# First MoE of a fused attention and two-MoE kernel: joining and casting the float64 weights at other turns

## The chip, the cores and the metric

One core of one Trainium2 chip runs the whole program in one launch. The metric is the device time of an execution in microseconds; lower is better.

## The reference

Three layers follow each other on 4 sequences of 576 tokens: causal attention with a local or a strided mask, a first MoE layer that is a plain two-matrix feed-forward net behind a layer norm, and a second MoE layer that sends each token to one of eight experts. The change touches the first MoE alone. Its two weight matrices are float64 (a float32 array times a float64 scalar), everything else is float32:

```python
def _moe_ref(x, g_ln, w_ch1, w_ch2) -> np.ndarray:
    mu = np.mean(x, axis=-1, keepdims=True)
    var = np.mean((x - mu) ** 2, axis=-1, keepdims=True)
    xn = (x - mu) / np.sqrt(var + 1e-06) * g_ln
    ch = np.maximum(xn @ w_ch1, 0.0) @ w_ch2
    return (x + ch).astype(np.float32)
```

Here w_ch1 is 512 x 2048 and w_ch2 is 2048 x 512; x is the attention's output, 2304 rows of 512.

## The kernel before

**The stages.** A prologue computes the attention of the first sequence. Then comes the first MoE over nine chunks of 256 tokens, c = 0 to 8, each with 16 groups f of 128 hidden columns. For a group, `mm1(c, f)` makes the hidden values in PSUM (12 matmuls, L645), ACT takes the relu of them as the high part h (L647), DVE makes the low part (L648), and `mm2(c, f)` multiplies both by w_ch2 and adds up in PSUM (12 matmuls, L661). Every product is of a high and a low part: high by high, high by low, low by high. The attention of the other three sequences is woven into the chunks, and behind them comes the second MoE.

**The order of the steps.** Chunks 0 and 1 run interleaved: a list `order` goes through (0,0), (0,1), (0,2), (1,0), (0,3), (1,1) and so on, with index t; (0, f) stands at t = 2f - 2, so that (0,14) is t = 26 and (0,15) t = 28. A step t first issues weight turns, then `mm1`, then the other work of the step, which is attention (scores L323 and L329, transposes L284 and L379, output L397 with its copies L415), layer norm (L533 to L634) and the `mm2` of the step before. A scheduler then sets each engine's order within what is pinned; the weight instructions are pinned by `keep`, so they do not overtake each other and what is pinned around them.

**The weights.** They come once, while chunks 0 and 1 run, in 32 blocks i of 512 KB: an even i is 128 columns of w_ch1 for group f = i/2, an odd i is 128 rows of w_ch2 for f = (i-1)/2. A block passes through these steps:

- `load_w` (L211): a DMA on SP's queue into half of a staging buffer `stg`, shared by blocks i and i+1. Staging pairs and the finished weight tiles w1_0 to w1_7 and w2_0 to w2_7 all come from one pool of 16 slots. At the end 15 tiles and the last staging pair (blocks 28 and 30) fill it, so w2_7 (blocks 29 and 31) gets the slot of that pair.
- `w_low` (L461, DVE): shifts the low words.
- `w_sign` (L467 and L468, ACT): two passes over the high words, which fix exponent and sign.
- `w_high` (L473, DVE): the join of high and low words. It reads what ACT's second pass wrote.
- `w_split`: a cast of the joined block to the high part (L487, ACT; on DVE for the first four blocks), and four POOL subtractions for the low part (L490), from the joined values and the cast.

**The turns.** The steps of a block sit in numbered turns. Two tables of lists, `turns` and `joins`, say what a turn issues. Before, block i is loaded at turn i - 4, has its low words shifted at i, its two ACT passes at i + 1, its join at the end of that same turn, and its cast and subtractions at i + 2. The last four blocks have a row of their own each. `weights_next` issues a turn and then its join:

```python
    def weights_next():
        weights_turn()
        weights_join()
```

In the prologue six turns are issued, one per unit of attention, with the joins one unit later. In the loop, step (0, f) goes on until turn 2f + 6 has been issued (for f = 14: until the last one), so most (0, f) steps issue two turns and the steps of chunk 1 none:

```python
        need = (2 * f + 4 + 2 * (f == 14) if f < 15 else len(turns)) + WA if t <= last[0] else 0
        while nw[0] < min(len(turns), max(need, W_START + int(WR * t))):
            weights_next()
```

Of the kernel before, what the change touches and what calls it, by code (L numbers as in the profile page):

```python
# [72 lines left out]
def attention_moe_moe(ctx: ExitStack, tc: tile.TileContext, q, k, v, g_ln, w_ch1, w_ch2, w_gate, w_local, w1, w2, out):  # L73
# [349 lines left out]
    NW, NSTG = 32, 6  # L423
# [67 lines left out]

    turns, joins = [[] for _ in range(NW + 3)], [[] for _ in range(NW + 3)]
    for i in range(NW):
        ld, lo, hi_, sp_ = i - NSTG + 2, i, i + 1, i + 2
        if i >= NW - 4:
            ld, lo, hi_, sp_ = ((27, 29, 30, 31), (23, 28, 29, 33), (27, 30, 31, 32), (23, 31, 32, 34))[i - NW + 4]
        if wide:
            turns[lo].append((w_low, i))  # L500
            turns[hi_].append((w_sign, i))
            joins[hi_].append((w_high, i))
        turns[sp_].insert(0, (w_split, i))
        if i >= NSTG:
            turns[ld].append((load_w, i))
    nw = [0]

    def weights_turn():
        for fn, i in turns[nw[0]]:
            fn(i)  # L510
        nw[0] += 1
# [3 lines left out]
    def weights_join():  # L515
        while joined[0] < nw[0]:
            for fn, i in joins[joined[0]]:
                fn(i)
            joined[0] += 1

    def weights_next():
        weights_turn()
        weights_join()


    lns, mus, xcs = {}, {}, {}
# [446 lines left out]
    for n in range(2):  # L973
        i = n * (NE + 129)
# [97 lines left out]
    for t, (c, f) in enumerate(order):  # L1072
# [3 lines that stand above are left out]
# [95 lines left out]
    def tab(n):  # L1171
        cur[0] += n
        return tb[:, cur[0] - n:cur[0]]
# [5 lines left out]
    sn, nx, fl, ld = tab(NTILE), tab(T1), tab(T1), tab(T1)  # L1179
# [455 lines left out]
```

## Time and profile before

| what | value |
|---|---|
| median of 3 runs | 872.17 us (872.1 to 872.27) |
| profiled execution | 872.77 us, span 870.6 us |
| PE busy | 845.5 us (97% of the span) |
| ACT busy | 353.4 us (41%) |
| DVE busy | 461.1 us (53%) |
| POOL busy | 171.8 us (20%) |
| granted TensorE clock | 0.995 of full speed, mean |

The span runs from the first to the last instruction of the profiled execution; some 2 us of its time lie outside. A row of the timeline gives start, duration, engine, line, operation, output and inputs, shape and count; a bracket gives the idle time of the engine ahead of the row and what ended it. PE is TensorE's matmul row; ACT, DVE and POOL are the scalar, vector and GpSimd engines.

### The profile page before, as it was taken

The page shows a single profiled execution, that of the slowest core. Times are in us where ns is not written, and L with a number is a line of the kernel's source. Part 1 is how long each engine was busy: PE and PEld are TensorE (multiplying, and loading weights), DVE is VectorE, ACT ScalarE, POOL GpSimd, SP SyncE. Part 2 cuts the span into 40 slices and gives each one's busy share as a digit, 9 for nine tenths or more (in the row PEclk, how much of TensorE's full clock was granted, in tenths as well). Part 3 has the DMA queues.
Part 4 walks back from the last instruction along what each step waited for, and adds up shares of the span by engine and source line. Part 5 has one row for each costly group of instructions (what it writes and reads, how often), then busy time and mean ns, then how long its engine had stood idle before and what let it go on. Part 6 is the DMA issues. An engine that isn't in the chain of part 4 may idle for free. (4 is left out here: it accounts for less than half of the span.)

```text
span 870.6 us, 18870 instructions
## 1 busy us (share of the span) xinstructions
PE 845.5 (97%) x7123; PEld 751.8 (86%) x7130; DVE 461.1 (53%) x1542; ACT 353.4 (41%) x857; POOL 171.8 (20%) x257
## 2 busy tenths in 40 slices
PE   9999899999999999999999999999999999999994
PEld 5688788899999999999999999999888868778773
DVE  4876765558656546666555464675815151121641
ACT  3787876633455233355211222242112252222551
POOL 2245542340120120120211212010032121120111
PEclk9999999999999999999999999999999999999998
DMA  9936352201221102210000000511266175354830
GB/s 192 253 122 202 106 169 74 50 11 54 66 47 42 50 17 59 51 26 16 26 2 26 2 25 1 195 37 38 100 229 243 62 255 213 145 188 169 303 119 23
DMA packets 96547, 87.17 MB, mean 100 GB/s; under 512 B 67378, under 2 KB 75574, under 8 KB 96440
## 3 DMA queue, kind: packets, MB, share of 16 engines
q1 hardware_dynamic: 89256, 69.61, 26.6%
q0 software_dynamic: 3552, 11.11, 3.7%
q10 hardware_dynamic: 3632, 5.09, 1.6%
q8 instruction: 59, 0.97, 0.5%
q14 instruction: 48, 0.39, 0.1%
HBM read 76.27 MB, written 9.97 MB: 99 GB/s over the span
## 5 line engine op out<-in xcount | busy, mean ns | idle before, releaser
L661 PE MATMUL acc<-h,w 128*128 128x256 f32 x1728 | 244.8, 289 | 2.1 <-DVE h L648 1.9
L645 PE MATMUL ps_h<-xc,w 128*128 128x256 f32 x1728 | 236.1, 285 | 0.0
L661 PEld LDWEIGHTS acc<-h,w 128*128 128x128 f32 x1728 | 217.9, 190 | 7.8 <-DVE h L648 3.2
L645 PEld LDWEIGHTS ps_h<-xc,w 128*128 128x128 f32 x1728 | 218.3, 192 | 1.8
L647 ACT ACTIVATE h<-ps_h 128x256 fp32r<-128x256 f32 x144 | 55.9, 389 | 215.7 <-PE ps_h L645 201.9
L648 DVE SCALAR_TENSOR_TENSOR h<-ps_h,h 128x256 fp32r<-128x256 f32 x144 | 60.4, 419 | 96.0 <-ACT h L647 95.5
L87 PE MATMUL ps_y<-wx,ht 128*128 128x512 f32 x336 | 83.8, 399 | 0.0
L490 POOL TENSOR_TENSOR w<-stg,w 128x128 fp32r<-128x128 f32 x128 | 62.5, 521 | 96.4 <-ACT w L487 57.5
L87 PE MATMUL ps_h<-wx,xs 128*128 128x512 f32 x336 | 81.1, 396 | 0.0
L87 PEld LDWEIGHTS ps_h<-wx,xs 128*128 128x128 f32 x336 | 62.7, 188 | 14.9
L87 PEld LDWEIGHTS ps_y<-wx,ht 128*128 128x128 f32 x336 | 61.0, 188 | 12.2 <-issue 0.2
L902 DVE TENSOR_TENSOR xs<-ps_tx,xs 128x512 fp32r<-128x512 f32 x14 | 9.7, 692 | 63.8 <-ACTq L1378 48.1
L1470 ACT ACTIVATE h<-ps_h 128x512 f32<-128x512 f32 x28 | 15.2, 595 | 56.6 <-PE ps_h L87 56.6
L791 DVE TENSOR_TENSOR wx<-raw,wx 128x1024 fp32r<-128x1024 f32 x32 | 37.3, 1217 | 1.3 <-ACT wx L788 1.3
L467 ACT ACTIVATE stg<-stg 128x512 f16<-128x512 f32 x27 | 37.1, 1374 | 0.0
L1484 DVE TENSOR_TENSOR ht<-ps_th,ht 128x512 fp32r<-128x512 f32 x28 | 18.4, 685 | 33.4 <-ACT ht L1483 33.3
L1508 POOL DMA_INDIRECT out_dram<-y,idx x14 | 17.8, 1271 | 90.6 <-ACT y L1507 81.8
L788 ACT CAST wx<-raw 128x1024 fp32r<-128x1024 f32 x32 | 31.8, 1060 | 5.6 <-PE acc L661 5.6
L359 ACT ACTIVATE sm<-sm,st 128x54 f32<-128x54 f32 (+1 forms) x80 | 27.6, 347 | 12.9 <-DVE st L347 12.8
L1483 ACT CAST ht<-ps_th 128x512 fp32r<-128x512 f32 x28 | 15.2, 590 | 36.3 <-PE ps_th L87 36.3
L881 POOL DMA_INDIRECT xg<-xrows,idx x15 | 16.1, 1074 | 53.5 <-issue 19.5
L1507 ACT ACTIVATE y<-ps_y,pr 128x512 f32<-128x512 f32 x18 | 12.4, 690 | 34.4 <-PE ps_y L1497 16.9
(397 smaller groups left out, 1189.1 us busy)
## 6 DMA issues: line engine op xcount, KB each, us to landing
raws<-in_moe_w_dram SPq DMA_DIRECT2D x20, 1024.0 KB
stg<-in_moe_w_ch_dram SPq DMA_DIRECT2D x32, 512.0 KB
raw<-in_moe_w_dram SPq DMA_DIRECT2D x16, 1024.0 KB
xrows<-row ACTq DMA_DIRECT2D x9, 520.0 KB
qnat<-in_q_dram SPq DMA_DIRECT2D x48, 72.0 KB
knat<-in_k_dram SPq DMA_DIRECT2D x48, 72.0 KB
v<-in_v_dram SPq DMA_DIRECT2D x24, 72.0 KB
v<-in_v_dram SPq DMA_DIRECT2D x72, 18.0 KB
```

Source lines behind the costliest of these rows:

```text
L87: return lambda *args, **kw: tc.keep_in_program_order(fn(*args, **kw))
L359: act.activation(sm[0:m, i, :], (ps if mode else sm)[0:m, i, :], AF.Exp, bias=st[0:m, 0, i:i + 1], scale=-1.0, **({} if mode else dict(acc ...
L467: keep(act.activation(t.bitcast(F16)[..., 1], f32(t[..., 1]), AF.Copy, scale=2.0 ** -112))
L490: keep(pool.tensor_tensor(o, x, f32(h), op=ALU.subtract))
L645: pe.matmul(ps, w[:, a, d, o:o + 128], xcs[c][:, b_, d, :], start=(i == 0), stop=(i == 11))
L647: act.activation(h[:, 0, :], ps, AF.Relu)
L648: dve.scalar_tensor_tensor(h[:, 1, :], ps, 0.0, f32(h[:, 0, :]), op0=ALU.max, op1=ALU.subtract)
L661: pe.matmul(accs[c][d // 2][:, d % 2, :], w[:, a, f % 2, d * 128:(d + 1) * 128], h[:, b_, :], start=(f == 0 and (a, b_) == (0, 0) and d % ...
L788: act.copy(wx[i][:, 0, :], raw[i // 2][:, i % 2, :])
L791: dve.tensor_tensor(wx[i][:, 1, :], raw[i // 2][:, i % 2, :], f32(wx[i][:, 0, :]), op=ALU.subtract)
L1484: dve.tensor_tensor(s_[1][:, 4 * g:4 * g + 4, :], ps, f32(s_[0][:, 4 * g:4 * g + 4, :]), op=ALU.subtract)
L1508: pool.indirect_dma_start(out=out, out_offset=bass.IndirectOffsetOnAxis(ap=places(s)[1], axis=0), in_=y, in_offset=None, bounds_check=NT - ...
```

## The change

Both tables get two more turns. A block's load goes from turn i - 4 to i - 2 and its cast and subtractions from i + 2 to i + 3. The join keeps its number, but `weights_next` now issues it ahead of the next turn, no longer behind its own. The last four blocks get new rows; their casts go from turns 31, 33, 32 and 34 to 33, 35, 34 and 36.

```diff
-    turns, joins = [[] for _ in range(NW + 3)], [[] for _ in range(NW + 3)]
+    turns, joins = [[] for _ in range(NW + 5)], [[] for _ in range(NW + 5)]
     for i in range(NW):
-        ld, lo, hi_, sp_ = i - NSTG + 2, i, i + 1, i + 2
+        ld, lo, hi_, sp_ = i - NSTG + 4, i, i + 1, i + 3
         if i >= NW - 4:
-            ld, lo, hi_, sp_ = ((27, 29, 30, 31), (23, 28, 29, 33), (27, 30, 31, 32), (23, 31, 32, 34))[i - NW + 4]
+            ld, lo, hi_, sp_ = ((28, 30, 31, 33), (24, 28, 29, 35), (28, 31, 32, 34), (24, 29, 30, 36))[i - NW + 4]
...
     def weights_next():
+        weights_join()
         weights_turn()
-        weights_join()
```

What the scheduler makes of it is seen in the engines' orders. In the rows below a bracket names the engines or DMA queues whose semaphores the instruction waits for, and the numbers behind names tell buffers apart.

ACT at the start of the loop, before: behind the first chunk's normalised input come the passes and casts of blocks 4 to 6 (L487 cast, L467 and L468 passes), the relus of (0,0) and (0,1) (L647) and the mean of chunk 1 (L555).

```order
L487 CAST w1_1_869<-stg_228 128x4x128 [waits DMAHW3_49,DMAHW1_49]
L467 ACTIVATE stg_228<-stg_228 128x512 [waits DMAHW1_49]
L564 ACTIVATE sq4_935<-xt0_379 128x1024
L468 ACTIVATE stg_228<-stg_228 128x512 [waits Activation_49]
L647 ACTIVATE h_894<-ps_h_881 128x256 [waits PE_49]
L647 ACTIVATE h_932<-ps_h_919 128x256 [waits PE_49]
L555 COPY mu_942<-ps_mu_937 128x256 [waits PE_49]
L487 CAST w2_1_897<-stg_228 128x512 [waits DMAHW3_49,DVE_49]
L467 ACTIVATE stg_640<-stg_640 128x512 [waits DMAHW7_49]
L297 ACTIVATE qT_153<-ps_tr_1292 128x288 [waits PE_49]
L468 ACTIVATE stg_640<-stg_640 128x512 [waits Activation_49]
L628 ACTIVATE xc_947<-xt1_419,g_sb_99 128x256 [waits DVE_49]
```

ACT at the same place, changed:

```order
L467 ACTIVATE stg_228<-stg_228 128x512 [waits DMAHW1_49]
L564 ACTIVATE sq4_926<-xt0_379 128x1024
L468 ACTIVATE stg_228<-stg_228 128x512 [waits Activation_49]
L647 ACTIVATE h_884<-ps_h_871 128x256 [waits PE_49]
L487 CAST w1_1_888<-stg_228 128x4x128 [waits DMAHW3_49]
L467 ACTIVATE stg_732<-stg_732 128x512 [waits DMAHW7_49,DVE_49]
L647 ACTIVATE h_923<-ps_h_910 128x256 [waits PE_49]
L468 ACTIVATE stg_732<-stg_732 128x512 [waits Activation_49]
L487 CAST w2_1_899<-stg_228 128x512 [waits DVE_49]
L467 ACTIVATE stg_732<-stg_732 128x512 [waits DMAHW0_49,DVE_49]
L555 COPY mu_933<-ps_mu_928 128x256 [waits PE_49]
L468 ACTIVATE stg_732<-stg_732 128x512 [waits Activation_49]
```

The mean of chunk 1 moved from ahead of the cast of block 5 to behind that cast and behind the passes of block 6 and the first pass of block 7.

ACT near the end of chunk 0, before: the relus of (0,14) and (1,12) are h_2590 and h_2618, ps_o_2538 and ps_o_2553 are the last two units of the second sequence's attention, and w2_7 takes blocks 29 and 31. The casts of blocks 28 and 30, into w1_7, stand 16 and 11 instructions ahead of the first row.

```order
L647 ACTIVATE h_2590<-ps_h_2577 128x256 [waits PE_49]
L415 COPY xt2_468<-ps_o_2538 128x12x6 [waits PE_49]
L415 COPY xt4_1809<-ps_o_2538 128x12x4 [waits DVE_49]
L647 ACTIVATE h_2618<-ps_h_2605 128x256 [waits PE_49,Activation_49]
L621 COPY rsb_2626<-ps_rs_2624 128x256 [waits PE_49]
L415 COPY xt2_468<-ps_o_2553 128x8x6 [waits PE_49]
L415 COPY xt4_1809<-ps_o_2553 128x8x4 [waits DVE_49]
L487 CAST w2_7_2566<-stg_1843 128x512 [waits Pool_49]
L487 CAST w2_7_2566<-stg31_1845 128x512
L647 ACTIVATE h_2653<-ps_h_2640 128x256 [waits PE_49,Activation_49]
```

ACT at the same place, changed; the last units of attention are now ps_o_2526 and ps_o_2541:

```order
L415 COPY xt2_468<-ps_o_2526 128x12x6 [waits PE_49]
L415 COPY xt4_1799<-ps_o_2526 128x12x4 [waits DVE_49]
L621 COPY rsb_2626<-ps_rs_2624 128x256 [waits PE_49]
L415 COPY xt2_468<-ps_o_2541 128x8x6 [waits PE_49]
L415 COPY xt4_1799<-ps_o_2541 128x8x4 [waits DVE_49]
L487 CAST w1_7_2555<-stg_2113 128x4x128 [waits Pool_49]
L487 CAST w1_7_2555<-stg_2113 128x4x128 [waits DVE_49]
L555 COPY mu_2729<-ps_mu_2727 128x256 [waits PE_49]
L487 CAST w2_7_2566<-stg_1846 128x512 [waits Activation_49,Pool_49]
L487 CAST w2_7_2566<-stg31_1848 128x512
L647 ACTIVATE h_2590<-ps_h_2577 128x256 [waits PE_49]
```

All four casts now stand behind the last attention copy, and the relus of (0,14) and (1,12) behind the casts; the cast of block 29 waits for POOL.

PE at that place, before: mm1(0,14) is ps_h_2577, mm1(1,12) is ps_h_2605, mm1(0,15) is ps_h_2640, and h_2510 feeds mm2(1,11).

```order
L397 MATMUL ps_o_2538<-pt_2518,v_2273 64x54 [waits DMAHW1_49,DMAHW7_49,DMAHW0_49,Activation_49]
L645 MATMUL ps_h_2577<-xc_853,w1_7_2393 128x256 x8
L645 MATMUL ps_h_2577<-xc_853,w1_7_2393 128x256 [waits Pool_49] x4
L661 MATMUL acc0_1110<-h_2510,w2_5_1833 128x256 x6
L397 MATMUL ps_o_2538<-pt_2518,v_2273 64x54 [waits DMAHW4_49,DMAHW3_49,DMAHW2_49]
L397 MATMUL ps_o_2538<-pt_2518,v_2273 64x54 x6
L661 MATMUL acc1_1111<-h_2510,w2_5_1833 128x256 x6
L645 MATMUL ps_h_2605<-xc_947,w1_6_1960 128x256 x5
L397 MATMUL ps_o_2553<-pt_2524,v_2469 64x54 [waits DMAHW6_49,DMAHW7_49,DMAHW5_49,Activation_49]
L645 MATMUL ps_h_2605<-xc_947,w1_6_1960 128x256 x7
L619 MATMUL ps_rs_2624<-dg_2621,mean_w_69 128x256 [waits Activation_49]
L645 MATMUL ps_h_2640<-xc_853,w1_7_2393 128x256 x2
```

PE at the same place, changed; h_2498 feeds mm2(1,11) in the last rows above these:

```order
L397 MATMUL ps_o_2526<-pt_2506,v_2267 64x54 x6
L397 MATMUL ps_o_2541<-pt_2512,v_2457 64x54 [waits DMAHW6_49,DMAHW7_49,DMAHW5_49,Activation_49]
L619 MATMUL ps_rs_2624<-dg_2621,mean_w_69 128x256 [waits Activation_49]
L619 MATMUL ps_rs_2723<-dg_2720,mean_w_69 128x256 [waits DVE_49,Activation_49]
L397 MATMUL ps_o_2541<-pt_2512,v_2457 64x54 [waits DMAHW2_49,DMAHW1_49,DMAHW0_49]
L397 MATMUL ps_o_2541<-pt_2512,v_2457 64x54 x2
L397 MATMUL ps_o_2541<-pt_2512,v_2457 64x36 x2
L553 MATMUL ps_mu_2727<-s__2684,mean_w_69 128x256 [waits Activation_49,Pool_49]
L645 MATMUL ps_h_2577<-xc_845,w1_7_2555 128x256 [waits Activation_49]
L645 MATMUL ps_h_2577<-xc_845,w1_7_2555 128x256 x7
L645 MATMUL ps_h_2577<-xc_845,w1_7_2555 128x256 [waits Pool_49] x4
L645 MATMUL ps_h_2605<-xc_938,w1_6_2095 128x256 x12
```

mm1(0,14), mm1(1,12) and mm1(0,15) moved from between the last attention units to behind them.

## Rows read from the trace of the kernel before

**Rows 1.** Stretches: us, mean, busy us (count) of PE, PEld, DVE, ACT, POOL; PEclk, DMA share, GB/s.

```profile
60.00:80.00 20.00, 18.45 (x146) 17.41 (x145) 15.29 (x37) 16.63 (x27) 12.18 (x22) 1.00 0.60 200
80.00:160.00 80.00, 74.48 (x761) 68.54 (x759) 50.83 (x141) 61.10 (x108) 32.17 (x69) 1.00 0.40 111
160.00:180.00 20.00, 18.85 (x180) 16.55 (x178) 7.53 (x22) 10.13 (x25) 7.84 (x16) 1.00 0.14 31
180.00:560.00 380.00, 379.81 (x3563) 367.26 (x3562) 224.16 (x866) 129.16 (x443) 50.05 (x50) 1.00 0.13 36
```

**Rows 2.** Groups by line, 50 to 185 us, ACT: count, busy us, mean ns, idle before.

```profile
L467 ACT ACTIVATE stg<-stg 128x512 f16<-128x512 f32 x27 | 37.1, 1374 | 0.0
L487 ACT CAST w<-stg 128x512 fp32r<-128x512 f32 x28 | 18.5, 664 | 10.6 <-DVE stg L473 9.4 <-DVE va L589 1.0
L468 ACT ACTIVATE stg<-stg 128x512 f32<-128x512 f32 x27 | 18.1, 670 | 0.3
```

**Rows 3.** Waits of DVE and ACT, 50 to 185 us: us in total, times, longest.

```profile
DVE stg L473 <- ACT stg L468: 12.6, 9, 2.8
...
ACT w L487 <- DVE stg L473: 9.4, 13, 1.8
```

**Rows 4.** Waits of PE, 55 to 185 us: us in total, times, longest.

```profile
PE ps_tr L284 <- ACT pt L387: 1.9, 2, 1.3
PE ps_tr L284 <- ACT qT L297: 1.6, 1, 1.6
PE acc L661 <- DVE h L648: 1.4, 2, 0.9
PE ps_pt L379 <- DVE sm L368: 1.1, 1, 1.1
```

**Rows 5.** Timeline at the start of the loop, DVE, ACT and PE.

```profile
56.76 0.38 ACT L555 COPY mu<-ps_mu 128x256 f32<-128x256 f32 x1
...
58.55 1.76 DVE L557 TENSOR_TENSOR xt<-xt,mu 128x512 f32<-128x512 f32 x2
...
57.00 1.84 PE L581 MATMUL ps_var<-mean_w,sq 128*128 128x1 f32 x16
...
61.64 1.60 PE L661 MATMUL acc<-h,w 128*128 128x256 f32 x12
63.08 1.72 PE L645 MATMUL ps_h<-xc,w 128*128 128x256 f32 x12
```

**Rows 6.** Timeline near the end of chunk 0, ACT, DVE, PE and POOL.

```profile
172.53 0.29 ACT L415 COPY xt<-ps_o 128x72 f32<-128x72 f32 x1 [0.93 <-PE ps_o L397]
172.85 0.34 DVE L415 COPY xt<-ps_o 128x96 f32<-128x96 f32 x1 [0.79 <-ACT xt L415]
...
173.22 0.25 ACT L415 COPY xt<-ps_o 128x48 f32<-128x48 f32 x1 [0.41 <-DVE xt L415]
...
175.12 0.60 PE L619 MATMUL ps_rs<-dg,mean_w 128*128 128x256 f32 x2
...
175.75 0.37 ACT L621 COPY rsb<-ps_rs 128x256 f32<-128x256 f32 x1
...
176.13 0.47 DVE L617 TENSOR_SCALAR dg<-iw,va 128x128 f32<-128x128 f32 x2
...
177.12 1.21 ACT L487 CAST w<-stg 128x512 fp32r<-128x512 f32 x2
...
177.86 3.43 POOL L490 TENSOR_TENSOR w<-stg,w 128x128 fp32r<-128x128 f32 x8 [0.28 <-ACT w L487]
...
180.12 0.38 ACT L647 ACTIVATE h<-ps_h 128x256 fp32r<-128x256 f32 x1 [1.79 <-PE acc L661]
...
181.40 0.43 DVE L648 SCALAR_TENSOR_TENSOR h<-ps_h,h 128x256 fp32r<-128x256 f32 x1
```

**Rows 7.** Instructions of L490 and of L473: duration ns least, median and most; first and last start.

```profile
L490 POOL TENSOR_TENSOR w<-stg,w x128: 457/470/1097, 35.0 to 180.8; 128x128 fp32r<-128x128 f32 x128
...
L473 DVE SCALAR_TENSOR_TENSOR stg<-stg x27: 661/693/886, 56.9 to 165.6; 128x512 int32<-128x512 int32 x27
```

## The prediction

> **What bounds the kernel now.** I read the stretches first. Between 180 and 560 us PE is busy for 379.81 of 380 us [rows 1], so whatever PE loses before 180 us reaches the end unchanged. Before that, in the stretches where the weights are made, it is idle for 1.55 us (60 to 80), 5.52 us (80 to 160) and 1.15 us (160 to 180): 8.2 us in all, and no change to the weights' turns can gain more than that. The granted clock is 1.00 throughout. ACT is the fullest of the other engines there (16.63 of 20 us, 61.10 of 80), and its weight work is the three groups of [rows 2]: 37.1 + 18.1 us of passes and 18.5 us of casts.
>
> Next come the waits. DVE stood in the join for ACT's second pass for 12.6 us, and ACT stood in the cast for the join for 9.4 us [rows 3]: the two engines hand a block to and fro inside a turn. But little of this is PE's: of PE's own waits, 1.4 us are for the low part of h and 1.1 us for DVE's softmax, and the two longest groups, 1.9 and 1.6 us, are transposes that wait for a PSUM buffer which ACT has to copy out [rows 4]. PE waits for the weights themselves nowhere in this list. So the change attacks waits that are long on DVE and ACT and short on PE, and pays with weights that come a turn later. The question is where a later weight meets PE.
>
> **Loads.** Of the 26 blocks that the tables load, 22 are loaded two turns later and shifted by DVE at the same turn as before; the last four are loaded one turn later, with their shifts moved too. Nothing is added on SP's queue. I cost it at nothing: in the order the loads keep their places among the attention's loads up to a few, and the staging slot, not the turn, lets most of them go. If that cover is gone, DVE stands in the shift of the low words; how long no row shows, so I take 0 and leave it to the range.
>
> **The start of the loop.** On ACT the mean of chunk 1 now stands behind the cast of block 5, both passes of block 6 and a pass of block 7. Before, its copy began at 56.76 [rows 5]. The added instructions are one cast (0.66), two long passes (2 x 1.37) and one short one (0.67) by [rows 2]: 4.1 us, so the mean is copied at about 60.9. DVE's subtraction of it, whose two halves took 1.76 us, can then not be before 61.3, and with ACT's and DVE's split of the first quarter chunk 1's first matmul group begins near 62.5 and is fed until about 64.7. Before, it ran from 63.08 to 64.8. It comes no later, then; but the 1.84 us of variance matmuls (from 57.00) stood ahead of it and stand behind it now. PE waits in their place: a loss of about 1.8 us. Part comes back, for 1.4 us of waits for h lie right behind in the old trace. I take a loss of 1.5 us, with 0 and 3 us as its ends.
>
> **The middle.** DVE no longer stands for ACT within a turn, and ACT hardly for DVE. What PE can get of it are its waits on DVE, 1.4 + 1.1 us [rows 4]; the transposes' 3.5 us hang on where ACT's copies stand, and in the changed order they still stand behind passes. I take a gain of 1.0 us. The ends: a gain of 4 us, if most of the 5.52 us goes, and a loss of 1.5 us, if ACT's copies fall behind by one more long pass.
>
> **The end of chunk 0.** Step t = 26 now issues turns 33 to 36, the casts of blocks 28, 30, 29 and 31, directly ahead of mm1(0,14), which needs block 28. Pinned as they are, they stand behind the last attention copies on ACT, and PE's order has put everything else ahead of mm1(0,14). Call Q the end of ps_o_2526 on PE.
>
> *From Q to P, the end of ps_o_2541.* PE's next matmul, ps_rs_2624, waits until Q's PSUM buffer is copied out: by ACT, DVE and ACT in turn, from 172.53 to 173.47 in the old trace, 0.95 us [rows 6]. Then ps_rs_2624 itself (two passes, 0.36), DVE's two scalings for the next one (0.47) and a start-up of about 0.1 us, after which PE goes on: 1.9 us after Q, in which it works for 0.25. Loss 1.6 us. Before, matmul groups of (0,14), (1,12) and (0,15) stood between these.
>
> *From P on* (times after P):
> - the same three copies, then the cast of block 28: its start 0.75, its end 1.4. mm1(0,14) starts, 8 matmuls at 0.12 (12 took 1.44 from 61.64 to 63.08 [rows 5]): 2.4;
> - POOL's low part: 8 subtractions took 3.43 [rows 6], 0.43 each, so block 28 is done at 3.15 and block 30 at 4.9. The last four matmuls follow the subtractions and end at 3.3, those of mm1(1,12) at 4.8;
> - the cast of block 29 writes the slot that blocks 28 and 30 are read from, so it waits for POOL until 4.9. Both casts (29 and 31) take 1.21: until 6.1;
> - the relu of (0,14) stands behind them on ACT: 0.38, until 6.5; its low part on DVE 0.43, until 6.95. Then mm2(0,14) can go: 11 further matmuls, until 8.3.
>
> In these 8.3 us PE had 36 matmuls and the mean to do, 4.4 us. Loss 3.9 us. Together 5.5 us at the end of chunk 0; the old trace has next to no idle time behind 168 us to set against it. Its ends are 2.5 us, if the cast of block 29 stood in nobody's way (mm2(0,14) then waits for POOL alone), and 7 us.
>
> Here a rule bears on the size. In the old trace a subtraction takes 470 ns at the median and up to 1097, and the join 661 to 886 [rows 7]: the two stretch each other at times. The Trainium skill, SBUF — State Buffer, Who interferes with whom, says that a DVE instruction with two SBUF inputs, as the join is, contends with a GpSimd instruction that reads SBUF, and that whoever comes second blocks fully. By this rule the join of block 30, due at 0.75 to 1.45, could hold up the first subtraction of block 28 by up to a join's 0.7 us, and the end would cost 6.2 us. I leave it out of the sum; the subtractions begin just as that join ends.
>
> **The sum.** 1.5 - 1.0 + 5.5 = 6.0 us slower. The profiled execution took 872.77 us, so it would take 878.8; the median of the runs is 0.6 us below the profiled one, so I predict 878.2 us.
>
> **The rivals.**
> - *The end costs less* (875 us or a little below). If ACT and DVE run so far ahead that the old trace's gaps in the middle go by 3 us and the end costs its lower 2.5 to 4 us, with 1.5 us at the start, the sum is +1 to +2.5: 873 to 875. For it: 22 us of waits leave DVE and ACT. Against it: the end is a chain of pinned instructions, which no lead shortens.
> - *Faster.* ACT decides PE's pace in 60 to 160 us, being busy there for 77.7 of 100 us, and the 9.4 us it no longer waits bring the attention's copies forward. Then the 7.07 us of PE's idle time there go almost whole, with no loss at the start. It decides if the end costs less than that gain: 7.0 - 3.5 gives 868.7. For it: ps_tr's 3.5 us are waits on ACT. Against it: in the changed order two of those copies stand behind a cast and a long pass.
> - *No change*, the start, middle and end cancelling: gain 4, loss 4, 872.2. Only with the middle at its better end.
> - *Weights late early on.* A turn is 4.2 us long on average (27 joins begin between 56.9 and 165.6 [rows 7]). If the blocks of the first groups have some 3 us of lead, a cast one turn later makes PE wait about 1 us for each of three of them: +3 on top, 881 to 884. Against it: a turn that waits for nobody is shorter, by up to the join's 0.7 us.
>
> **How the numbers follow.** About 0.2%, 1.74 us, is what a measurement of this kernel can tell from no change: 870.4 to 873.9. Chances: the forecast (875 to 881) 0.62; the cheaper end 0.14, a third of it within the 0.2%; faster 0.12; no change 0.05; weights late 0.07. So faster 0.12, same 0.10, slower 0.78. The range leaves out the faster case and the worst of the late weights: 872.5 to 882.
>
> **What would show it.** Right: PE idle 5 us or more in the 20 us around the end of chunk 0, in three gaps (ahead of ps_rs, of mm1(0,14) and of mm2(0,14)), with the cast of block 29 released by POOL; DVE's wait for ACT in the join near nothing; 2 to 3 us of PE idle at 56 to 80; no idle from there to 560 us. Wrong: if mm2(0,14) follows mm1(1,12) without a gap, or PE's idle time between 80 and 160 falls below 2 us.

## The result and the profile after

The changed kernel takes 877.27 us (median of 6 runs, 876.5 to 880.99) and the kernel before 872.22 us (median of 6): a ratio of 1.0061, 95% interval 1.0045 to 1.0077, 5.05 us slower. The profiled execution took 876.93 us with a span of 875.0; the forecast was 878.8 for a profiled execution and 878.2 for the median.

First the stretches of the changed kernel, as in [rows 1] (us, mean, busy us and count of PE, PEld, DVE, ACT, POOL; PEclk, DMA share, GB/s):

```profile
60.00:80.00 20.00, 17.30 (x138) 16.41 (x136) 17.50 (x38) 19.41 (x32) 15.51 (x27) 1.00 0.43 141
80.00:160.00 80.00, 75.43 (x776) 69.53 (x777) 52.96 (x139) 58.45 (x104) 35.58 (x67) 1.00 0.46 126
160.00:180.00 20.00, 16.67 (x148) 14.10 (x143) 8.24 (x22) 8.79 (x22) 5.82 (x10) 0.83 0.13 30
180.00:560.00 380.00, 378.92 (x3553) 365.98 (x3553) 221.80 (x860) 129.44 (x443) 52.23 (x55) 1.00 0.12 32
```

PE's idle time is 2.70 us in 60 to 80 (before 1.55), 4.57 in 80 to 160 (5.52), and 3.33 + 1.08 behind 160 (1.15 + 0.19). And a number has moved that the forecast did not look at: the granted clock of 160 to 180 us is 0.83, where it was 1.00. In finer stretches:

```profile
170.00:175.00 5.00, 2.68 (x14) 1.51 (x14) 1.31 (x5) 1.21 (x6) 0.10 (x1) 0.70 0.14 33
175.00:180.00 5.00, 4.05 (x21) 3.88 (x22) 2.12 (x3) 1.46 (x4) 5.00 (x9) 0.62 0.13 31
180.00:185.00 5.00, 4.02 (x31) 3.62 (x31) 0.93 (x3) 2.37 (x6) 4.24 (x10) 1.00 0.00 0
```

So TensorE ran at its lower level, 1.2 GHz, for 6.8 us from 172.0 on. Just before, PE had waited 0.89 us, and a second wait, of 0.67 us, was under way. The waits, against [rows 3] and [rows 4] (us in total, times, longest), first of DVE:

```profile
DVE stg L473 <- ACT stg L468: 2.6, 4, 1.3
```

of ACT:

```profile
ACT w L487 <- POOL w L490: 2.6, 1, 2.6
ACT w L487 <- DVE stg L473: 1.5, 1, 1.5
```

and of PE:

```profile
PE ps_tr L284 <- ACT pt L387: 2.1, 3, 0.9
PE ps_tr L284 <- ACT qT L297: 2.0, 2, 1.5
PE ps_mu L553 <- POOL s__2684 L533: 1.8, 1, 1.8
PE acc L661 <- DVE h L648: 1.6, 1, 1.6
PE acc L661 <- ACT h L647: 0.9, 1, 0.9
PE ps_rs L619 <- ACT xt L415: 0.9, 1, 0.9
PE ps_h L645 <- ACT xc L628: 0.8, 1, 0.8
PE ps_rs L619 <- DVE dg L617: 0.7, 1, 0.7
```

DVE's 12.6 us of waiting in the join are 2.6 now, and ACT's 9.4 us in the cast are 1.5 plus one wait of 2.6 for POOL. PE got little of these 15 us: its transposes wait as long as before, and four waits at the end of chunk 0 are new. The new waits stand in the timeline of PE like this (start, duration, then in brackets the idle time ahead and what ended it):

```profile
169.16 0.78 PE L397 MATMUL ps_o<-pt,v 54*64 54x54 f32 x18
170.83 0.70 PE L619 MATMUL ps_rs<-dg,mean_w 128*128 128x256 f32 x2 [0.89 <-ACT xt L415]
172.20 1.19 PE L619 MATMUL ps_rs<-dg,mean_w 128*128 128x256 f32 x2 [0.67 <-DVE dg L617]
173.32 0.86 PE L397 MATMUL ps_o<-pt,v 54*64 54x54 f32 x10
175.95 1.22 PE L553 MATMUL ps_mu<-s__2684,mean_w 128*128 128x256 f32 x2 [1.77 <-POOL s__2684 L533]
176.61 4.22 PE L645 MATMUL ps_h<-xc,w 128*128 128x256 f32 x24
181.73 2.04 PE L661 MATMUL acc<-h,w 128*128 128x256 f32 x12 [0.90 <-ACT h L647]
```

and ACT, POOL and DVE beside it:

```profile
174.88 1.21 ACT L487 CAST w<-stg 128x512 fp32r<-128x512 f32 x2
...
180.19 1.21 ACT L487 CAST w<-stg 128x512 fp32r<-128x512 f32 x2 [2.61 <-POOL w L490]
181.30 0.38 ACT L647 ACTIVATE h<-ps_h 128x256 fp32r<-128x256 f32 x1
...
174.90 0.99 POOL L533 TENSOR_TENSOR s__2684<-s__2684,xt 128x256 f32<-128x256 f32 x1 [10.16 <-DVE xt L415]
175.86 4.30 POOL L490 TENSOR_TENSOR w<-stg,w 128x128 fp32r<-128x128 f32 x8
...
177.61 1.80 DVE L557 TENSOR_TENSOR xt<-xt,mu 128x512 f32<-128x512 f32 x2 [2.30 <-ACT mu L555]
```

The casts of blocks 28 and 30 start at 174.88, POOL has both low parts at 180.16, the cast of block 29 starts at 180.19 behind it, and mm2(0,14) follows the relu at 181.73.

### The profile page after: what moved, and what is told of

It is laid out like the page before. It is cut to its first block, busy times and chain, and to the rows that moved or that the text cites. A ratio compares the mean times of both kernels' runs of the same rounds, so it can differ in the third digit from the quotient of the medians.

```text
span 875.0 us, 18876 instructions
## 1 busy us (share of the span) xinstructions
PE 846.8 (97%) x7123; PEld 752.8 (86%) x7130; DVE 465.3 (53%) x1542; ACT 354.5 (41%) x857; POOL 179.6 (21%) x257
## 5 line engine op out<-in xcount | busy, mean ns | idle before, releaser
L647 ACT ACTIVATE h<-ps_h 128x256 fp32r<-128x256 f32 x144 | 55.6, 386 | 211.8 <-PE ps_h L645 200.0
L490 POOL TENSOR_TENSOR w<-stg,w 128x128 fp32r<-128x128 f32 x128 | 70.7, 584 | 84.6 <-ACT w L487 42.0
L467 ACT ACTIVATE stg<-stg 128x512 f16<-128x512 f32 x27 | 37.5, 1387 | 0.6 <-DVE stg L461 0.6
L359 ACT ACTIVATE sm<-sm,st 128x54 f32<-128x54 f32 (+1 forms) x80 | 27.6, 347 | 12.8 <-DVE st L347 12.7
```

The costliest lines, as they stand in the source:

```text
L359: act.activation(sm[0:m, i, :], (ps if mode else sm)[0:m, i, :], AF.Exp, bias=st[0:m, 0, i:i + 1], scale=-1.0, **({} if mode else dict(acc ...
L467: keep(act.activation(t.bitcast(F16)[..., 1], f32(t[..., 1]), AF.Copy, scale=2.0 ** -112))
L490: keep(pool.tensor_tensor(o, x, f32(h), op=ALU.subtract))
L647: act.activation(h[:, 0, :], ps, AF.Relu)
```

## The experiments

Five theories were set against each other. **A**: the loss is the end of chunk 0, where the last four casts stand directly ahead of mm1(0,14). **B**: it is the general rule, each cast a turn later. **C**: it is the join's place ahead of the next turn. **D**, formed after the first four runs: it is TensorE's lower clock, which follows idle time of PE. **E**, formed after D had failed in part: the lower clock follows a wait of PE together with matmuls that stream a single column. Theories A to C are about the place of the loss, D and E about its kind; they can hold side by side.

All results, each against runs of the kernel before taken beside it. The last three columns are from each kernel's profile, which shows a single execution: PE's idle time in 60 to 185 us, the time in 44 to 200 us at 1.2 GHz, and how much later than in before's profile (240.82 us) the mean of chunk 3 is copied, which tells what is lost by then.

| kernel | median us (runs) | ratio to before, 95% | idle | 1.2 GHz | later by |
|---|---|---|---|---|---|
| before | 872.22 (6) | | 8.2 | 0 | 0 |
| the change | 877.27 (6) | 1.0061 (1.0045 to 1.0077) | 11.6 | 6.8 | 4.6 |
| late_four | 878.37 (5) | 1.0068 (1.0055 to 1.0081) | 11.4 | 6.8 | 4.8 |
| general_only | 875.43 (8) | 1.0037 (1.0023 to 1.0051) | 8.8 | 6.8 | 3.3 |
| join_only | 878.54 (6) | 1.0074 (1.0059 to 1.0089) | 9.0 | 10.2 | 5.2 |
| end_one_step_earlier | 875.16 (7) | 1.0027 (1.0016 to 1.0038) | 9.1 | 6.8 | 3.0 |
| general_filled | 874.16 (11) | 1.0021 (1.0011 to 1.0030) | 7.0 | 0 | 1.0 |
| join_filled | 880.10 (5) | 1.0087 (1.0073 to 1.0101) | 11.0 | 3.4 | 6.0 |
| end_low_on_dve | 877.21 (5) | 1.0047 (1.0034 to 1.0061) | 10.3 | 10.2 | 4.5 |
| change_filled | 878.42 (5) | 1.0064 (1.0050 to 1.0077) | 9.1 | 10.2 | 6.6 |
| change_filled_low_on_dve | 876.78 (5) | 1.0046 (1.0033 to 1.0060) | 8.2 | 10.2 | 5.0 |
| one_step_earlier_filled | 875.54 (6) | 1.0034 (1.0022 to 1.0046) | 6.9 | 6.8 | 3.5 |
| general_var_spread | 872.67 (11) | 1.0005 (0.9995 to 1.0016) | 9.0 | 0 | 0.0 |
| before_var_spread | 872.33 (11) | 0.9998 (0.9989 to 1.0007) | 7.0 | 3.4 | -0.2 |

In the rows with "filled" the zero matmuls count as busy, though they do no work.

**The parts alone.** `late_four`: the kernel before, the four rows of casts changed.

```diff
-((27, 29, 30, 31), (23, 28, 29, 33), (27, 30, 31, 32), (23, 31, 32, 34))
+((27, 29, 30, 33), (23, 28, 29, 35), (27, 30, 31, 34), (23, 31, 32, 36))
```

> The kernel before, with only the casts of the last four blocks at the change's turns (33, 35, 34, 36); everything else as before. Theory A (the loss is the end of chunk 0, where these four casts stand directly ahead of mm1(0,14)): 876.5 to 878 us, 4 to 6 us slower, with PE idle at least 3 us between 165 and 185 us and the clock below 1.00 in part of that stretch, as in the changed kernel. Theory B (the loss is the general rule, a cast one turn later for all blocks): within 1 us of 872.2. Theory C (the loss is the join ahead of the next turn's instructions): within 1 us of 872.2.

Measured: 878.37 us, 5.9 us above the 872.49 of before beside it. Its profile has the same end as the change's; below the stretches, the relu of (0,14) on ACT and mm2(0,14) on PE:

```profile
170.00:175.00 5.00, 3.02 (x35) 1.94 (x34) 0.81 (x4) 1.13 (x4) 0.00 (x0) 1.00 0.14 33
175.00:180.00 5.00, 3.82 (x16) 3.64 (x17) 2.08 (x3) 1.67 (x4) 4.60 (x9) 0.53 0.13 31
...
181.59 0.37 ACT L647 ACTIVATE h<-ps_h 128x256 fp32r<-128x256 f32 x1
...
182.26 1.78 PE L661 MATMUL acc<-h,w 128*128 128x256 f32 x12
```

These four numbers alone make a loss as large as the change's, a little above what A had: theory A. The clock falls here too, from about 175.3 us, in the third of the waits. But the relu ends at 181.96 us, behind the casts, and mm2(0,14) starts at 182.26: of this delay the slower matmuls can have made 0.3 us at most, and the chain of casts and subtractions the rest.

`general_only`: the change, but with the last four blocks' shifts, passes and casts at before's turns.

```diff
-((28, 30, 31, 33), (24, 28, 29, 35), (28, 31, 32, 34), (24, 29, 30, 36))
+((28, 29, 30, 31), (24, 28, 29, 33), (28, 30, 31, 32), (24, 31, 32, 34))
```

> The changed kernel, with the shifts, passes and casts of the last four blocks at the turns of before (casts at 31, 33, 32, 34; only their loads stay at 28 and 24); the general rule and the join's new place stay. Theory A: 871 to 872.7 us, because by the changed trace PE is 0.4 us ahead when it first uses block 27; little idle time at 165 to 185 us and clock 1.00 there. Theory B: 876 to 878 us. Theory C: 876 to 878 us.

Measured: 875.43 us, 2.9 above before, above what A allows and below what B or C want. But its idle time is only 0.6 us more than before's. What is new stands in the stretches,

```profile
88.00:92.00 4.00, 4.00 (x42) 3.72 (x41) 1.24 (x4) 0.38 (x1) 0.00 (x0) 0.99 0.90 284
92.00:96.00 4.00, 4.00 (x23) 3.93 (x21) 3.90 (x16) 2.94 (x4) 2.54 (x4) 0.59 0.38 144
170.00:174.00 4.00, 4.00 (x27) 3.68 (x23) 0.33 (x1) 1.14 (x4) 0.00 (x0) 0.57 0.19 43
```

and in PE's timeline, where twelve matmuls that take 1.6 us at the higher clock take 2.3 and 2.5:

```profile
86.38 0.47 PE L284 MATMUL ps_tr<-iw,knat 96*128 96x96 f32 x3 [1.46 <-ACT qT L297]
...
89.62 1.95 PE L581 MATMUL ps_var<-mean_w,sq 128*128 128x1 f32 x16
91.43 2.53 PE L661 MATMUL acc<-h,w 128*128 128x256 f32 x12
93.75 2.28 PE L645 MATMUL ps_h<-xc,w 128*128 128x256 f32 x12
```

Half of 6.8 us is 3.4 us: with 0.6 us of idle time it more than covers the 3.3 us that chunk 3 comes later. By this reading the general rule costs clock, not waits; `general_var_spread` below tests it. The losses of the two parts do not add up to the change's: its profile has the idle time and the fall at the end, but no fall near 92. Its eight runs go the same way, if not strictly: 872.92 us at a mean granted clock of 0.995, 875.4 at 0.992, 878.16 at 0.989, but also 876.52 at 0.993 and 874.5 at 0.991.

`join_only`: the kernel before with `weights_join()` ahead of `weights_turn()`, and nothing else.

> The kernel before, with only the join issued ahead of the next turn and no longer behind its own; no turn number is changed. Theory A: within 0.8 us of 872.2, with DVE's wait for ACT's second pass in the join partly gone and ACT's wait for the join in the cast still there, since the cast now follows the join directly. Theory B: the same. Theory C: 876 to 878 us.

Measured: 878.54 us, 6.1 above before: C alone had a loss here, of 876 to 878. Yet the idle time is 0.8 us more than before's, ACT's wait for the join in the cast is 12.8 us (9.4 before), and 10.2 us pass at 1.2 GHz. The longest such stretch, from 89.3 to 96.2 us, begins in the middle of the variance matmuls of chunk 1, which here also had a wait ahead of them:

```profile
88.20 2.58 PE L581 MATMUL ps_var<-mean_w,sq 128*128 128x1 f32 x16 [1.50 <-DVE kT L293]
90.64 2.91 PE L661 MATMUL acc<-h,w 128*128 128x256 f32 x12
```

So swapping the two calls is not harmless by itself, though it takes hardly any time of PE directly.

`end_one_step_earlier`: the change, with turns 33 to 36 issued at step (0,13).

```diff
-        need = (2 * f + 4 + 2 * (f == 14) if f < 15 else len(turns)) + WA if t <= last[0] else 0
+        need = (2 * f + 4 + 2 * (f == 14) + 4 * (f == 13) if f < 15 else len(turns)) + WA if t <= last[0] else 0
```

> The changed kernel, with its turns 33 to 36 issued one step of chunk 0 earlier, at (0,13) in place of (0,14). Theory A: the casts leave the chain ahead of mm1(0,14), and most of the 5 us comes back: 871.5 to 874 us; the cast of block 29 still waits for POOL, but then ahead of work that has a step of time. Theory B: 876 to 878 us. Theory C: 876 to 878 us.

Measured: 875.16 us, 2.7 above before, between the theories' ranges: 2.4 us less loss than the change's 5.05, as A wants, but not the 871.5 to 874 that A named. What is left is as in general_only, with a stretch at 1.2 GHz near 92 us and another from 167.0 to 170.4 (there from 170.4 to 173.8). A repair of the end brings the change down to what its general rule costs, and not further.

**The clock.** `general_filled` and `join_filled` put zero matmuls into idle time of PE, with a `nil` tile of zeros; `keep` pins them, and in `general_filled` also half of the key transposes, behind three of them. The line that adds them:

```diff
+            keep(pe.matmul(accs[min(accs)][0].rearrange("p d t -> p (d t)")[:, 0:256], nil[:, 0:128], nil, start=False, stop=False))
```

> The kernel of general_only, with three matmuls of a zero tile that add zero to the accumulator put where PE idled in its profile: inside mm2(0,3), after its first matmul (1.63 us idle at 74), and ahead of the second half of the key transposes (1.46 us idle at 86). Every other matmul stands where it stood. In that profile PE's idle time is 0.5 us more than before's, but the granted clock is 0.5 (1.2 GHz) from 91.9 to 95.9 us and again from 170.3 to 173.6. Theory D (what the general rule costs is the lower clock that follows idle time of PE, not the idle time): the first of the two stretches at 1.2 GHz is gone or rarer, and the median falls by about half of the 3.4 us, to 873 to 874.5 us, though PE has more to do. If the idle time itself is what costs: no gain, 875.4 us or up to 0.8 us above it, as the zero matmuls fill only time in which PE waited.

Measured: 874.16 us, 1.3 below general_only, with no stretch at 1.2 GHz in its profile, and five of its 11 runs at 872.8 to 873.1. As D had it, though the intervals of the two ratios overlap.

> The kernel of join_only, with four matmuls of a zero tile that add zero to the accumulator put ahead of the variance matmuls of chunk 1, where PE idled for 1.5 us at 86.7 to 88.2 in its profile; 1.2 GHz was granted there from 89.3 to 97.0 us. Every other matmul stands where it stood. Theory D: that stretch at 1.2 GHz is gone or rarer, and the median falls by 2 to 3.5 us, to 875 to 876.5 us; the second one (132.9 to 138) stays. If the idle time itself is what costs: 878.5 us or up to 0.5 us above it.

Measured: 880.10 us, which neither foresaw. The long stretch at 1.2 GHz is gone, but the experiment was not clean: DVE's order changed too, the softmax moved in between the steps of the layer norm, and PE got a new wait, right behind which (from 101.2 us) 3.4 us at 1.2 GHz are left.

```profile
PE ps_sc L336 <- DVE sm L356: 2.8, 1, 2.8
```

`change_filled` and `one_step_earlier_filled` carry the same six zero matmuls as general_filled.

> The changed kernel, with the six zero matmuls of general_filled at the same two places; every other matmul stands where it stood. This takes out the clock's fall near 92 us, which the changed kernel's profile did not have but its other runs, at a lower mean clock, may; the fall at the end of chunk 0 stays. Theory D: 875.5 to 876.8 us. If falls near 92 us play no part in the changed kernel: 877 to 877.8 us.

> The kernel of end_one_step_earlier, with the same six zero matmuls. With the casts of the last blocks out of the chain and the fall near 92 us gone, what is left against before is the fall at 160 to 185 us and the start of the loop: 873 to 874.3 us by theories A and D; 875 us or more if the clock is not the cause.

Measured: 878.42 us, above both ranges, and 875.54, in the range that spoke against the clock: no better than without the zero matmuls. But in both profiles the clock falls near 92 all the same; of the change:

```profile
92.00:96.00 4.00, 4.00 (x22) 4.00 (x22) 3.67 (x15) 3.00 (x4) 2.13 (x4) 0.57 0.65 223
```

So D does not hold as it was put: filling the waits of 74 and 86 us does not reliably hold the clock at 92. (Whether zero matmuls act on the clock as others do, no run shows.) What stood unchanged just ahead of the fall in all these profiles were the variance matmuls, 16 rows of one column in 1.95 us, in which PE counts as busy. That gave theory E and its test. In the kernel before, the same matmuls stand in a row too, with no wait near them and no fall.

`general_var_spread` and `before_var_spread`: these matmuls put one by one between those of mm2(0,5).

```diff
-        for d, a, b_ in terms:
...
+        for k, (d, a, b_) in enumerate(terms):
+            if (c, f) == (0, 5) and 2 <= k < 10:
+                var_k.pop(0)()
...
```

> The kernel of general_only, with the variance matmuls of chunk 1 (16 rows of one column each, 1.95 us in a row from 89.62 in its profile) put one by one between the matmuls of mm2(0,5) that follow them; on ACT, POOL and SP nothing moves. Filling idle time with zero matmuls did not keep the clock up near 92 us, and in each profile with the fall the variance matmuls end just before it. Theory E (the clock falls behind a stretch in which PE waits and then streams single columns): no stretch at 1.2 GHz between 88 and 98 us, and the median falls by 1 to 1.7 us from 875.4, over what the same edit gives to the kernel before. If it is idle time alone: as general_only, 874.9 to 876 us, fall near 92 us still there.

> The kernel before, with the same edit: the variance matmuls of chunk 1 put one by one between those of mm2(0,5); nothing else moves on any engine. Its profile has no fall of the clock there. By theory E and by the other alike: no change or little, 871.5 to 872.5 us; what it gains here is to be taken off the gain of general_var_spread.

Measured: 872.67 us for the general rule, 2.8 below general_only, and 872.33 for the kernel before, 0.3 below it: both within 0.2% of before. The profile of general_var_spread, which shows its fastest execution (871.73 us):

```profile
80.00:160.00 80.00, 75.55 (x781) 69.73 (x780) 52.41 (x138) 58.44 (x105) 34.96 (x67) 1.00 0.45 126
160.00:180.00 20.00, 18.22 (x172) 16.50 (x171) 8.27 (x23) 10.00 (x24) 5.73 (x12) 1.00 0.13 29
```

The waits that end at 73.9 us (1.6 us) and at 85.9 (1.47) are still there, idle time is 0.8 us more than before's, and the clock is 1.00. So the loss of general_only was, by these medians, the clock, and the single columns in a row had a part in bringing it on at 92. The gain is larger than the 1.0 to 1.7 us foreseen, because the profiled execution has no fall near 170 either, although PE waits 1.78 us there; four of its 11 runs, at 873.8 to 875.5 us and a mean clock of 0.991 to 0.994, may have had one. What decides over that second fall is open.

As a rule E is not shown. Three other stretches at 1.2 GHz on record, of join_only, join_filled and before_var_spread in this order:

```profile
133.70:137.10 3.40, 3.40 (x30) 3.08 (x28) 1.73 (x4) 1.35 (x3) 0.21 (x1) 0.50 0.38 86
101.20:104.50 3.30, 3.30 (x17) 3.30 (x16) 2.38 (x7) 1.95 (x6) 0.87 (x3) 0.50 0.00 0
59.70:63.10 3.40, 3.40 (x19) 3.40 (x17) 3.26 (x7) 3.40 (x8) 2.65 (x4) 0.50 0.19 43
```

The first two follow waits of 1.83 and 2.80 us with no single columns near; the third follows the single columns of chunk 0 with no wait above 0.4 us near. And the change's own profile has a wait of 1.48 us and the single columns, from 84 to 91 us, without a fall. Join_only's loss is open too: that its clock fell amid the same matmuls is seen, but not tried by this edit.

**The chain at the end.** `end_low_on_dve`: the change, with the four subtractions of block 30 on DVE.

```diff
-            keep(pool.tensor_tensor(o, x, f32(h), op=ALU.subtract))
+            keep((dve if i == NW - 2 else pool).tensor_tensor(o, x, f32(h), op=ALU.subtract))
```

> The changed kernel, with the low part of block 30 (four subtractions) made by DVE in place of POOL. In the changed kernel's profile POOL has block 28 ready at 177.58 and block 30 at 180.16, and only then can the cast of block 29 start, since it takes the slot both are read from; DVE has nothing to do at 175.3 to 177.6. Theory A (the end is a chain: cast 28, POOL, cast 29, cast 31, relu, mm2(0,14)): cast 29 starts at 177.6 to 178 in place of 180.19, and 1.5 to 2.5 us come back: 874.8 to 875.8 us. If the chain is elsewhere (PE's own work at 1.2 GHz from 172 to 179 sets the pace): within 0.7 us of 877.3.

Measured: 877.21 us, no gain. In its profile the chain did shorten: the second pair of casts starts 3.13 us after the first, no longer 5.31, and mm2(0,14) follows mm1(1,12) without a wait. On ACT

```profile
176.01 1.22 ACT L487 CAST w<-stg 128x512 fp32r<-128x512 f32 x2
...
179.14 1.25 ACT L487 CAST w<-stg 128x512 fp32r<-128x512 f32 x2 [0.43 <-DVE w L490]
```

and on PE

```profile
177.74 4.55 PE L645 MATMUL ps_h<-xc,w 128*128 128x256 f32 x24
182.13 1.60 PE L661 MATMUL acc<-h,w 128*128 128x256 f32 x12
```

From the first use of block 27 to the last mm2 of chunk 0 it takes 21.55 us in place of 22.99. But this execution also had the fall near 92 that the change's profile lacks (10.2 us at 1.2 GHz in place of 6.8), which, at half of its 3.4 us, costs 1.7 us. So the pair was compared once more with the zero matmuls in both.

> The kernel of change_filled, with the low part of block 30 made by DVE in place of POOL. In the profile of end_low_on_dve the stretch from the first use of block 27 to the last mm2 of chunk 0 was 1.4 us shorter than in the changed kernel, but its clock fell near 92 us as well, and its median was no better. Theory A with D: 1 to 1.8 us below change_filled, 874 to 875.5 us. If the cast of block 29 does not matter: as change_filled.

Measured: 876.78 us against 878.42, 1.6 below: the difference is inside the 1 to 1.8 foreseen, the time above the 874 to 875.5. Both profiles have the same 10.2 us at 1.2 GHz. By the profiles the wait of the cast of block 29 for the slot is worth about 1.5 us; the medians bear it out less firmly, as the five runs of each overlap (875.52 to 877.49 and 876.76 to 878.95) and the first pair showed 0.1. With the wait gone, PE's own work at 1.2 GHz (24 matmuls in 4.55 us) sets the pace.

## Why the prediction was right, and where it was not

The sum, 6.0 us, against 5.05 measured, was right in sign and near in size. By its terms:

- **Start of the loop, +1.5.** Measured +1.15 (2.70 for 1.55 us idle in 60 to 80), near in size but not part by part. The mean of chunk 1 was copied at 59.77, not at 60.9, and PE waited for its normalised input 0.75 + 0.34 us where 1.8 had been reckoned. The waits for h, which were to give part back, did not: 1.4 us before, 1.6 now. The variance matmuls moved behind, as said.
- **The middle, -1.0.** Measured -0.95 (4.57 for 5.52). Of the 15 us that DVE and ACT no longer wait, PE gets this one microsecond, since its longest waits are for ACT's copies in the transposes, and these did not move. That kills the rival "faster", which would have had 7 us of it.
- **The end, +5.5.** Of the 4.6 us that chunk 3 comes later in the profile, the two terms above leave 4.4 us for it. The chain is the one forecast, but its parts are not. From Q to P PE idled 0.89 + 0.67 us; 1.6 had been reckoned. The cast of block 28 began 0.70 us after P, for 0.75. From there on each step came later than listed: block 30 was done 6.0 us after P, not 4.9, and the relu ended at 7.5, not 6.5. Two items on POOL were missing: the sum for the mean of chunk 2 (L533, 0.99 us) got in ahead of the subtractions, and PE's ps_mu waited 1.77 us for it ahead of mm1(0,14); and the subtractions of block 30 took 2.63 us for 1.74, as DVE's L557 ran beside them.
- **The failing step** is "The granted clock is 1.00 throughout", which was read from before's profile and carried over as if the change could not touch it. It let the whole loss be written as idle time. The sign promised, "PE idle 5 us or more in the 20 us around the end", did not come: idle grew by 3.1 us behind 160 (to 4.4 us), and PE was busy for longer with the same matmuls at 1.2 GHz.

What this fall costs in the change is another matter. Ahead of P it lengthened the chain: the second ps_rs took 1.19 us for 0.60 [rows 6], and the ten matmuls of L397 behind it 0.86 us, for this in the kernel before:

```profile
175.88 0.54 PE L397 MATMUL ps_o<-pt,v 54*64 54x54 f32 x10
```

That is 0.9 us. Behind P it mostly took the place of waiting. The 24 matmuls of mm1(0,14) and mm1(1,12) took 4.22 us, and PE still waited 0.90 us for the relu, which stood behind ACT's casts and POOL's subtractions. At 0.12 us each they would have been done 1.3 us sooner (an estimate), and PE would have waited for the same relu that much longer. So the end costs its chain, as forecast, and the clock a smaller part of it; no run takes this fall away alone, and its price stays open. That a chain longer than listed and a fall that was not foreseen came out 1.1 us below the 5.5 is not taken apart here: that the total came so near was partly luck.

The rule weighed there was the one on who blocks whom. In the old reckoning the join of block 30 was to meet the first subtraction of block 28; it ended at 175.31, before the subtractions began, and block 28's four took 0.43 us each. By the Trainium skill, SBUF — State Buffer, Who interferes with whom, a DVE instruction with two SBUF inputs contends with GpSimd's reads. The trace agrees for another pair: L557 reads two tiles from SBUF. Here are the two subtractions that began beside it (ns at least, median and most), its own two halves, and its halves later in the program:

```profile
L490 POOL TENSOR_TENSOR w<-stg,w x2: 907/908/909, 178.0 to 178.8; 128x128 fp32r<-128x128 f32 x2
L557 DVE TENSOR_TENSOR xt<-xt,mu x2: 931/940/948, 177.6 to 178.5; 128x512 f32<-128x512 f32 x2
L557 DVE TENSOR_TENSOR xt<-xt,mu x12: 684/688/693, 245.8 to 536.8; 128x512 f32<-128x512 f32 x12
```

The other two subtractions of block 30 took 0.46 us each. Two of four doubled, and both halves of L557 grew by 0.25 us: these times fit engines that stop for each other in turn, as the rule quoted in the prediction has it, though no row shows the stop itself. What the prediction left out of its sum, at 0.7 us, came with this pair at 0.9 us. In the old trace, too, the longest subtraction (1097 ns, at 66.2 us) lay beside L634 and not beside a join, where the longest was 0.92 us.

The rival "weights late early on" did not come (no wait of PE for a weight before 160 us). "The end costs less" did not either: late_four alone costs 5.9 us.

## What to carry to other kernels

Slack that is taken from engines off the critical path is worth what the bound engine waits for them, here 1 us of 15. A later turn cost PE little idle time until the last items of the list, where no work was left to stand in between, so look at the end of a pipelined list first. When a change moves the waits of a PE that is 97% busy, read the granted clock by stretch in both profiles, and look at what PE did before a fall: in general_only, spreading the variance matmuls took 2.8 us off the median with the waits left in place. And see whether the slower matmuls are on the path: in the change PE waited behind them all the same. Compare medians of several runs, and look at each run's mean clock, before an edit of 0.3% is called good or bad.

## What was not expected of the hardware

- The clock fell to 1.2 GHz behind single waits of PE of 0.9 us (the change, at 172 us) to 2.8 us (join_filled, at 101), once with no wait near (before_var_spread, at 59.7), and did not fall behind a wait of 1.58 us in the kernel before (near 128 us) nor behind 1.78 us in general_var_spread. What decides is open.
- Executions of one and the same kernel differ in it: general_only ran from 872.92 to 878.16 us, at mean clocks of 0.995 to 0.989.
- DVE and POOL slowed each other when both read SBUF: 0.91 us for a subtraction that takes 0.46 otherwise, 0.94 for a half of L557 that takes 0.69.
- A fall does not always cost what it takes. In the profile of before_var_spread TensorE ran at 1.2 GHz from 59.7 to 63.1 us, behind the variance matmuls of chunk 0, and the execution still took 872.1 us: PE idled 1.2 us less in 60 to 185 than before's profile, so it seems that work that comes later found less to wait for.
